# A RWKV attention and MLP kernel on one core: a new issue order, and DMA turns of rows and keys for the last eight tiles

## The chip, the cores and the metric

The kernel runs on one core of a Trainium2 chip. A core has five engines that run side by side, each working through its own queue of instructions in order: TensorE (PE, matrix products, with the loading of its weights shown apart as PEld), VectorE (DVE), ScalarE (ACT), GpSimd (POOL) and SyncE (SP, which here only issues DMAs). Data moves between the device's memory and the on-chip memory by 16 DMA engines. Engines wait for each other through semaphores. The metric is the device time of one execution in microseconds (us); the kernel before took 156.52 us, the median of 3 runs (156.29 to 156.55).

## The reference

Inputs are r, k, v of shape (4, 8, 768, 48), that is batch, heads, time and head width, per-head vectors w and u, a norm weight g and two matrices of an MLP (384×1536 and 1536×384), all in 32 bits.

```python
for t in range(S):
    cur = np.einsum('bhd,bhe->bhde', u[None] * kt, vt)
    y[:, :, t] = np.einsum('bhd,bhde->bhe', rt, state + cur)
    state = w[None, :, :, None] * state + np.einsum('bhd,bhe->bhde', kt, vt)
...
mu, var = mean and variance of x over its 384 columns
xn = (x - mu) / np.sqrt(var + 1e-06) * g_ln
out = x + np.maximum(xn @ w_ch1, 0.0) @ w_ch2
```

Here x is y with the eight heads side by side: 4 × 768 rows of 384.

## The kernel before

**Tiles.** The 768 steps of a sequence are cut into six chunks of 128; with four sequences there are 24 tiles of 128 rows, numbered 0 to 23, each with 384 columns (8 heads of 48). Within a chunk the recurrence is written as a masked product, and a state of 48×48 per head is carried from chunk to chunk.

**Steps.** The kernel is written as small functions, one for each step of the work, and a list, `PLAN`, that calls them. An entry `SK,5,g` calls the function SK for tile 5 on GpSimd; `v` is VectorE, `s` ScalarE, and `-` stands where the engine is fixed. The order of the list is the order in which each engine gets its instructions; between engines only the semaphores count. Nothing else decides the order. For one tile the steps are:

- LK, LR, LV: SP loads keys, rows r and values (192 KB each).
- SK, SR: keys and rows are scaled by powers of w (`Fk`, `Fr`) into `sck` and `scr`, in 16 bits. CV: the values in 16 bits.
- TR: TensorE turns `scr` and `sck` (128×128 transposes, four each) into the bank `tr`; TC (or TCr and TCk for the halves) copies the result to `trs`. For tiles in `K_BY_DMA` TR turns only the rows, TCr copies them, and TKD lets a DMA turn the keys straight into `trs`, issued by SP.
- Q: product of turned rows and keys. AT: TensorE forms the 128×128 products of keys and rows for each head. AM masks them into `A` (AMa and AMb do a half each).
- S: TensorE forms the coefficients of u and, but for the last chunk of a sequence, the increment of the state; for the tiles in `ZPE` it also adds the state before through the identity. CC copies the coefficients, ZU and ZD make the next state `Z`. VB: coefficients times values, on GpSimd.
- Y: TensorE forms the output of the attention from `A`, the values and the state. X adds `Vb`: this is x.
- ST, AG: mean and variance. XN: mean minus x, in 16 bits, `xn`. RS: the inverse root of the variance, used at the end (the sign and g go into the first matrix).
- LT: TensorE turns `xn` (three 128×128 transposes) into the bank `tr`, and XT copies it to `xT`. LTD, which the plan of before does not call, lets a DMA turn `xn` straight into `xT`, issued by SP.
- UP, RL, DN: the MLP. `GROUPS` puts tiles into groups of one or two. UP,16g+m computes four (two, in a group of two) blocks of 128 hidden units of group g for all rows of the group, into one of two banks `hp`; RL takes the positive part into `hT`. DN,4i+d adds the d-th third of the hidden units to the output of tile i; there are three of them a tile. OT multiplies by RS and adds x, STO stores.

**Start.** MW, MP and MI set up constants, WF and ROWSI load w and u (ROWSI by four small DMAs on ScalarE's queue, into `u_p` and `w_p`), LN, WBM, FK and FR make the powers of w, LW1 and SW load and scale the thirds of the first matrix (`w_f`, `w_sb`), IW2 loads those of the second with a cast, on GpSimd's queue. WU and DU are dummy products on TensorE, as many as the number says.

**Buffers.** `SLOTS` says how many buffers each tile has: 10 for each of the three inputs, 3 for `sck`, `scr`, `trs` and `xn`, 4 for `xT` and `hT`. A step that writes into a buffer waits until its last reader is done.

Lines that the prediction names: L203 (products by a vector or tile: SK, SR, Q, ZD), L261 (dummies), L338 (TR), L357 (AT), L367 (AM), L458 and L460 (XN), L477 (TKD), L482 (LT), L497 (UP), L513 and L515 (RL on ScalarE and on VectorE), L525 (DN), L535 (OT), L542 (STO). L198 and L200 are copies on ScalarE and on the other two engines.

Of the kernel before, what the change touches and what calls it, by code (L numbers as in the profile page):

```python
# [10 lines left out]
ACT = mybir.ActivationFunctionType  # L11
ENG = mybir.EngineType

GROUPS = [1, 1, 1, 1, 1, 1, 1, 1, 2, 2, 2, 2, 2, 2, 1, 1, 1, 1]
ZPE = [1, 2, 3]
K_BY_DMA = [18, 19, 20, 21, 22, 23]
SLOTS = {'kf': 10, 'rf': 10, 'vf': 10, 'sck': 3, 'scr': 3, 'vv': 4, 'trs': 3, 'q': 2, 'A': 2, 'cc': 4, 'Z': 3, 'ZS': 2, 'Vb': 3, 'x': 13, 'xn': 3, 'xT': 4, 'hT': 4, 'ot': 3}
PLAN = """
MW,0,v WF,0,- TL,0,s MI,0,g MP,0,v WU,13,- MM,0,g LN,0,s LK,0,- ROWSI,0,s WBM,0,- LV,1,-
LR,0,- FK,0,s CV,1,v FR,0,s SK,0,v LK,1,- SR,0,g LR,1,- SK,1,v DU,18,- TR,0,- UW,0,g  # L20
WL,0,s LK,2,- SR,1,g TCk,0,s LR,2,- TCr,0,s SK,2,g Q,0,v DU,22,- TR,1,- LV,0,- AT,0,-
TCk,1,s SR,2,v LG,0,- LW1,2,- TCr,1,s AMa,0,v CV,0,g UGC,0,s AMb,0,v DU,13,- TR,2,- S,0,-
Q,1,v TC,2,s Y,0,- AT,1,- CC,0,v ZU,0,v LV,2,- AMa,1,v VB,0,g DU,3,- S,1,- SW,7,s
AMb,1,v LW1,1,- SW,8,s IW2,0,g X,0,v SW,6,s DU,13,- AT,2,- Q,2,v Y,1,- CV,2,g ST,0,v
AG,0,v LW1,0,- CC,1,s XN,0,s RS,0,g ZU,1,v SW,5,s SW,3,v DU,16,- LT,0,- VB,1,g XT,0,v
SW,4,s DU,6,- UP,2,- X,1,v S,2,- RL,2,s SW,2,g ST,1,v UP,1,- SW,0,s SW,1,v IW2,2,g
AG,1,v AM,2,v UP,0,- XN,1,s IW2,1,g LK,3,- LT,1,- RL,1,s CC,2,v XT,1,v LR,3,- DU,1,-
Y,2,- RL,0,s VB,2,g ZU,2,v UP,18,- SK,3,v LV,3,- DN,0,- SR,3,v RL,18,s UP,17,- X,2,v
TR,3,- CV,3,g ST,2,v RL,17,s UP,16,- RS,1,g TC,3,v AG,2,v RL,16,s Q,3,v AT,3,- XN,2,v
RS,2,g AM,3,v S,3,- LT,2,- DN,1,- XT,2,s CC,3,s UP,33,- ZU,3,v LK,4,- DN,2,- LV,6,-  # L30
VB,3,g UP,32,- OT,0,v Y,3,- SK,4,v LR,4,- DN,4,- RL,32,v RL,33,s DN,5,- CV,6,s LR,5,-
X,3,v SR,4,v DN,6,- LV,4,- ST,3,v TR,4,- SR,5,g UP,34,- OT,1,v LV,5,- TC,4,s AG,3,v
DN,8,- CV,4,v XN,3,g LK,5,- Q,4,v AT,4,- RL,34,s DN,9,- RS,3,g AM,4,v LK,7,- LT,3,-
S,4,- XT,3,s DN,10,- LK,6,- SK,5,v CC,4,s VB,4,g UP,48,- OT,2,v LR,10,- TR,5,- SK,7,v
UP,49,- SK,6,g ZU,4,v RL,48,s LR,6,- TC,5,v Y,4,- CV,5,s DN,12,- RL,49,v LR,12,- ZD,4,g
AT,5,- X,4,v DN,13,- AM,5,v LR,7,- SR,6,g UP,50,- LV,7,- ST,4,v TR,6,- RL,50,s Q,5,v
SR,7,g Y,5,- AG,4,v STO,1,- TC,6,v S,5,- XN,4,s DN,14,- STO,0,- CC,5,v CV,7,s Q,6,v
VB,5,g LT,4,- LV,11,- AT,6,- XT,4,v S,6,- OT,3,v UP,64,- LV,9,- X,5,v CC,6,s UP,66,-
RS,4,g ST,5,v RL,64,s LR,8,- TR,7,- AM,6,v RL,66,s UP,65,- SR,10,g CV,9,s LK,11,- DN,16,-
AG,5,v RL,65,s TC,7,v RS,5,g Y,6,- LR,9,- XN,5,s DN,17,- ZU,6,v VB,6,g Q,7,v LT,5,-  # L40
LK,8,- DN,18,- XT,5,s AT,7,- X,6,v LK,10,- UP,80,- ST,6,v S,7,- SR,8,v RL,80,s LR,14,-
UP,82,- SK,8,g AM,7,v UP,81,- RL,82,s LK,9,- TR,8,- CC,7,s AG,6,v OT,4,v RL,81,s RS,6,g
Y,7,- LK,14,- TC,8,v XN,6,s DN,20,- VB,7,g CV,11,s ZU,7,v LV,8,- LT,6,- DN,21,- Q,8,v
SR,9,g X,7,v XT,6,s AT,8,- LK,15,- SK,9,v DN,22,- CV,8,s UP,96,- ZD,7,g LV,13,- ST,7,v
AM,8,v TR,9,- RL,96,s SK,10,g STO,2,- S,8,- UP,97,- LR,11,- CC,8,s TC,9,v SR,12,g Y,8,-
OT,5,v RL,97,s TR,10,- STO,4,- Q,9,v AT,9,- VB,8,g LK,12,- TC,10,s AG,7,v UP,98,- ZU,8,v
AM,9,v ZD,8,g S,9,- LV,12,- XN,7,s DN,24,- CC,9,s LT,7,- Q,10,v SK,11,g LR,16,- DN,25,-
ZU,9,v RL,98,s X,8,v AT,10,- XT,7,s LV,15,- DN,26,- ZD,9,g ST,8,v UP,114,- AM,10,v LV,10,-
VB,9,g Y,9,- RL,114,s UP,113,- STO,3,- SR,11,g AG,8,v X,9,v XN,8,s LK,13,- UP,112,- CV,10,s
ST,9,v RS,7,g TR,11,- OT,6,v RL,112,s LR,17,- S,10,- AG,9,v TC,11,v RL,113,s SR,14,g Y,10,-  # L50
DN,28,- CC,10,s LR,15,- SK,13,v CV,12,s XN,9,s VB,10,g LT,8,- AT,11,- ZU,10,v LK,17,- DN,29,-
XT,8,s Q,11,v SK,12,g LT,9,- X,10,v DN,30,- LV,16,- XT,9,s AM,11,v S,11,- UP,130,- RS,8,g
LR,13,- UP,129,- CC,11,v OT,7,v RL,130,s ZD,10,g LK,21,- TR,12,- ST,10,v RL,129,s UP,132,- CV,13,v
VB,11,g TC,12,s SR,15,v LK,19,- UP,131,- RL,132,s Y,11,- STO,6,- SR,13,v AT,12,- RL,131,s LK,16,-
Q,12,v UP,128,- AG,10,v X,11,v XN,10,g S,12,- STO,5,- RL,128,s TR,13,- ST,11,v LK,22,- UP,133,-
CV,15,v SR,16,v SK,15,g DN,32,- TC,13,v RL,133,s LR,22,- DN,33,- AG,11,v AM,12,v XN,11,s Q,13,g
LR,21,- LT,10,- CC,12,s DN,34,- XT,10,s ZU,12,v Y,12,- LV,21,- SK,14,g LT,11,- OT,8,v AT,13,-
S,13,- XT,11,v DN,36,- LR,19,- VB,12,g AM,13,v TR,14,- CV,16,g LR,20,- UP,144,- CC,13,v X,12,v
TC,14,s RS,9,g DN,37,- ZU,13,v LV,14,- RL,144,s ST,12,v ZD,13,g UP,145,- STO,7,- UP,148,- RL,145,s
VB,13,g LV,20,- Q,14,v AT,14,- RL,148,s Y,13,- LK,18,- SK,16,v TR,15,- AG,12,v DN,38,- CV,14,v  # L60
TC,15,v LV,22,- UP,149,- OT,9,v XN,12,s TR,16,- LV,23,- Q,15,v RL,149,s DN,40,- X,13,v SR,19,g
LV,17,- ST,13,v UP,147,- TC,16,s AM,14,v UP,146,- LV,19,- RL,147,s LT,12,- CV,17,g S,14,- AG,13,v
RL,146,s XT,12,v AT,15,- LR,18,- CC,14,v Y,14,- XN,13,s SK,17,v DN,41,- ZU,14,v LR,23,- Q,16,v
LT,13,- DN,42,- VB,14,g AM,15,v XT,13,s LK,20,- S,15,- ZD,14,g UP,163,- OT,10,v STO,8,- UP,162,-
RL,163,s X,14,v SR,18,g DN,44,- SK,18,v SR,17,g UP,160,- ST,14,v STO,9,- AT,16,- RL,162,s CC,15,v
AG,14,v Y,15,- LK,23,- AM,16,v RL,160,s RS,10,g TR,17,- CV,19,s UP,164,- VB,15,g LV,18,- TC,17,v
UP,165,- RL,164,s SR,20,g ZU,15,v DN,45,- Q,17,v XN,14,s STO,10,- ZD,15,g TR,18,- S,16,- X,15,v
TCr,18,s DN,46,- ST,15,v UP,161,- AG,15,v OT,11,v Y,16,- RL,161,s SR,21,v XN,15,g AT,17,- TKD,18,-
CV,20,s LT,14,- CC,16,v DN,48,- XT,14,v RL,165,s VB,16,g LT,15,- DN,49,- XT,15,v Q,18,v RS,11,g
UP,180,- X,16,v STO,11,- ZU,16,v DN,50,- SK,19,g ST,16,v S,17,- TR,19,- OT,12,v UP,176,- RL,180,s  # L70
ZD,16,g AG,16,v CC,17,s DN,52,- AM,17,v VB,17,g UP,178,- RL,176,s TKD,19,- SK,20,g DN,53,- XN,16,v
RL,178,s Y,17,- STO,12,- CV,18,g UP,177,- TCr,19,s AT,18,- CV,21,s Q,19,g TR,20,- RL,177,s X,17,v
UP,181,- AM,18,v DN,54,- RL,181,s SR,22,g UP,179,- OT,13,v TKD,20,- SR,23,g AT,19,- ST,17,v RL,179,s
S,18,- DN,56,- TCr,20,v AG,17,v LT,16,- XN,17,s RS,12,g Y,18,- DN,57,- XT,16,v CC,18,s CV,22,s
ZU,18,v LT,17,- VB,18,g DN,58,- XT,17,v AM,19,v UP,197,- STO,13,- Q,20,g TR,21,- UP,192,- X,18,v
OT,14,v S,19,- AT,20,- RL,197,s SK,22,v DN,60,- TCr,21,s UP,195,- ST,18,v CC,19,s ZU,19,v DN,61,-
VB,19,g STO,14,- AM,20,v Y,19,- RL,195,s ZD,19,g S,20,- DN,62,- X,19,v RL,192,s TR,22,- CV,23,s
Y,20,- OT,15,v SK,21,g UP,194,- ST,19,v CC,20,s UP,193,- TCr,22,v RL,194,s TKD,22,- AG,19,v TR,23,-
VB,20,g RL,193,s UP,196,- AG,18,v XN,18,s TCr,23,v DN,64,- TKD,21,- XN,19,g X,20,v RL,196,s LT,18,-
DN,65,- RS,13,g XT,18,v STO,15,- AT,21,- SK,23,g ZU,20,v LT,19,- DN,66,- XT,19,v AM,21,v ZD,20,g  # L80
UP,212,- UP,209,- RL,212,s Q,21,g OT,16,v Y,21,- UP,208,- RL,209,s AT,22,- S,21,- Q,22,g AM,22,v
DN,68,- CC,21,s UP,213,- VB,21,g ZU,21,v RL,208,s DN,69,- ST,20,v RL,213,s STO,16,- ZD,21,g UP,211,-
# [500 lines left out]
```

## Time and profile before

| | |
|---|---|
| time, median of 3 runs | 156.52 us (156.29 to 156.55) |
| the profiled execution | 156.55 us, span 154.4 us |
| UP (L497) | 648 matmuls, 57.2 us busy |
| DN (L525) | 288 matmuls, 57.1 us busy |
| RL on ScalarE (L513) | 68, 40.0 us busy |
| AM (L367) | 26, 29.1 us busy |
| VB on GpSimd (L420) | 24, 21.6 us busy |
| TR, rows (L338) | 96 transposes, 9.7 us busy |
| moved by DMA | 23.51 MB, 152 GB/s |

The span runs from the first to the last instruction. Busy time counts an engine's instructions; those of TensorE overlap one another, so their sum is longer than the time in which they follow each other. In the slices of the profile each digit stands for a fortieth of the span, 3.86 us, and gives its busy share in tenths. A row of the timeline has start, duration, engine, line, operation, the tiles written and read, the count, and in brackets the idle time before it and what ended that. A row for a line or a tile gives the shortest, the median and the longest duration in ns.

### The profile page before, as it was taken

What the parts mean: (1) busy time and instruction counts of PE and PEld (TensorE: products, weight loads), DVE (VectorE), ACT (ScalarE), POOL (GpSimd) and SP (SyncE); (2) the same over time, 40 slices, a digit from 0 to 9 for tenths busy, and PEclk for the clock granted to TensorE, in tenths of its full rate; (3) what the DMA queues carried; (4) which work ended last, traced back from release to release, by engine and by line L of the source; (5) the groups of instructions that cost most, each with busy time, mean ns of one, the idle gap of its engine ahead of it and who ended that gap; (6) DMA issues with size and microseconds to landing.
All of it is one profiled execution on the core that took longest, in us unless ns stands there. A gap on an engine that the chain in (4) does not pass through costs nothing.

```text
span 154.4 us, 4697 instructions
## 1 busy us (share of the span) xinstructions
PE 146.4 (95%) x1926; PEld 118.6 (77%) x1926; DVE 119.4 (77%) x242; ACT 76.2 (49%) x149; POOL 95.7 (62%) x135
## 2 busy tenths in 40 slices
PE   7689999999899999999999999999999999999990
PEld 4488788868677887979688878877778778878770
DVE  2256989789998999999999999797797769734211
ACT  4526884434155747657535746356455244143330
POOL 3182665356749499995693698798766968333200
PEclk9999999999999999999999999999999999999998
DMA  4999999999999999989899897132153051102111
GB/s 82 192 182 354 349 200 206 210 177 212 226 200 188 199 255 179 257 170 232 170 243 208 176 261 107 51 89 34 51 87 87 0 89 51 51 20 82 56 56 51
DMA packets 84487, 23.51 MB, mean 152 GB/s; under 512 B 79857, under 2 KB 82930, under 8 KB 84466
## 3 DMA queue, kind: packets, MB, share of 16 engines
q1 hardware_dynamic: 83202, 22.03, 64.5%
q0 software_dynamic: 432, 1.18, 4.2%
q8 instruction: 15, 0.25, 0.7%
q10 hardware_dynamic: 832, 0.00, 0.3%
q14 instruction: 6, 0.05, 0.1%
HBM read 18.88 MB, written 4.72 MB: 153 GB/s over the span
## 4 chain that ended last, share of the span: by engine, by line
PE 73%; DVE 16%; DMA 3%; ACT 2%; issue 2%; SPq 1%; POOL 1%; POOLq 0%; DVEq 0%; ACTq 0%
PE o L525 27%; PE hp L497 26%; PE tr L338 5%; PE at L357 4%; DVE A L367 4%; DMA rf<-in_r_dram 3%; PE tr L482 3%; DVE scr L203 2%; PE y L438 2%; PE s L401 2%; PE y L430 2%; PE o L261 2%; DVE x L445 2%; PE s L388 1%; DVE stats L448 1%
## 5 line engine op out<-in xcount | busy, mean ns | idle before, releaser
L513 ACT ACTIVATE hT<-hp 128x512 bf16<-128x512 f32 x68 | 40.0, 597 | 49.5 <-PE hp L497 48.9
L497 PE MATMUL hp<-xT,w_sb 128*128 128x128 bf16 (+1 forms) x648 | 57.2, 237 | 0.3 <-ACT w_sb L306 0.2
L525 PE MATMUL o<-w_sb,hT 128*128 128x384 bf16 x288 | 57.1, 326 | 0.2 <-DVE hT L515 0.2
L497 PEld LDWEIGHTS <-w_sb 128*128 128x128 bf16 x648 | 49.4, 113 | 4.4 <-ACT w_sb L306 0.4
L525 PEld LDWEIGHTS <-hT 128*128 128x128 bf16 x288 | 25.3, 98 | 11.6 <-DVE hT L515 0.4
L367 DVE TENSOR_TENSOR A<-at,mask 128x1024 bf16<-128x1024 f32 (+1 forms) x26 | 29.1, 1127 | 3.3 <-PE at L357 3.3
L420 POOL TENSOR_TENSOR Vb<-vf,cc 128x384 f32<-128x384 f32 x24 | 21.6, 898 | 12.6 <-ACT cc L198 6.7
L203 POOL TENSOR_TENSOR scr<-rf,Fr 128x384 bf16<-128x384 f32 x16 | 16.2, 1019 | 11.7 <-DMA rf<-in_r_dram 8.2
L535 DVE SCALAR_TENSOR_TENSOR ot<-o,rs,x 128x384 f32<-128x384 f32 x24 | 14.7, 611 | 10.3 <-PE o L525 10.2
L445 DVE TENSOR_TENSOR x<-y,Vb 128x384 f32<-128x384 f32 x24 | 13.1, 547 | 4.2 <-POOL Vb L420 3.1
L203 POOL TENSOR_TENSOR Z<-ZS,WLZ 128x384 bf16<-128x384 f32 x13 | 13.6, 1048 | 2.5 <-DVE ZS L414 2.3
L198 ACT COPY trs<-tr 128x512 bf16<-128x512 bf16 (+1 forms) x13 | 10.0, 782 | 10.5 <-PE tr L338 10.5
L448 DVE BATCH_NORM_STATS2 stats<-x 128x6 f32<-128x384 f32 x24 | 13.3, 554 | 0.4
L203 POOL TENSOR_TENSOR sck<-kf,Fk 128x384 bf16<-128x384 f32 x12 | 12.6, 1046 | 0.3 <-PE s L401 0.3
L469 POOL TENSOR_TENSOR rs<-rs,expo 128x1 f32<-128x1 f32 (+1 forms) x18 | 10.9, 603 | 1.5
L338 PE MATMUL tr<-ident,scr 128*128 128x128 bf16 x96 | 9.7, 227 | 1.9 <-POOL scr L203 1.9
L261 PE MATMUL o<-warm 128*128 128x128 bf16 x105 | 10.3, 269 | 1.0 <-DVE warm L226 1.0
L203 DVE TENSOR_TENSOR sck<-kf,Fk 128x384 bf16<-128x384 f32 x12 | 9.6, 799 | 1.4 <-DMA kf<-in_k_dram 1.4
L203 DVE TENSOR_TENSOR q<-trs 128x512 bf16<-128x512 bf16 x18 | 8.8, 489 | 2.4 <-ACT trs L198 2.4
L261 PEld LDWEIGHTS <-warm 128*128 128x128 bf16 x105 | 8.7, 124 | 2.4 <-issue 1.3
L458 ACT ACTIVATE xn<-x,mv 128x384 bf16<-128x384 f32 x15 | 9.2, 613 | 2.5 <-DVE mv L452 2.5
L357 PE MATMUL at<-trs 48*128 48x128 bf16 x192 | 9.8, 222 | 0.4 <-DVE trs L200 0.3
(66 smaller groups left out, 180.2 us busy)
## 6 DMA issues: line engine op xcount, KB each, us to landing
kf<-in_k_dram SPq DMA_DIRECT2D x24, 192.0 KB, 3.9
vf<-in_v_dram SPq DMA_DIRECT2D x24, 192.0 KB, 4.1
rf<-in_r_dram SPq DMA_DIRECT2D x24, 192.0 KB, 3.9
out_dram<-ot SPq DMA_DIRECT2D x24, 192.0 KB, 2.5
w_f<-in_moe_w_ch_dram SPq DMA_DIRECT2D x3, 768.0 KB, 7.3
w_sb<-in_moe_w_ch_dram POOLq DMA_DIRECT2D x3, 384.0 KB, 6.5
trs<-sck SPq DMA_TRANSPOSE x6, 3.6
u_p<-in_u_dram ACTq DMA_DIRECT2D x2, 0.8 KB, 3.1
```

Of the source, the lines that this page charges most:

```text
L203: engines[e].tensor_tensor(out=out, in0=in0, in1=in1, op=ALU.mult)
L261: nc.tensor.matmul(out=warm_ps[0][:, :P], lhsT=warm[:], rhs=warm[:], start=True, stop=True)
L338: nc.tensor.transpose(out=t[:, a * HP + q, :], in_=flat[:, q, :], identity=ident[:])
L357: nc.tensor.matmul(out=t[:, par, q, :], lhsT=trs(i)[p0 : p0 + D, 1, q, :], rhs=trs(i)[p0 : p0 + D, 0, q, :], start=True, stop=True,)
L367: nc.vector.tensor_tensor(out=AA(i)[:, a:b].rearrange("p e q t -> p (e q) t"), in0=psum["at", i][:, a:b].rearrange("p e q t -> p (e q) t") ...
L420: nc.gpsimd.tensor_tensor(out=Vb(i)[:].rearrange("p (h d) -> p h d", h=H), in0=vf(i)[:], in1=cc(i)[:].unsqueeze(2).to_broadcast([P, H, D]) ...
L445: nc.vector.tensor_tensor(out=xx(i)[:], in0=psum["y", i][:, :C], in1=Vb(i)[:], op=ALU.add)
L448: nc.vector.bn_stats(out=stats[i % 4][:], in_=xx(i)[:])
L497: nc.tensor.matmul(out=t[:, a * gw : (a + 1) * gw], lhsT=w1_sb[n][kc][:, fb::FB], rhs=xT(g)[:, kc, :gw], start=(kc == 0), stop=(kc == CK - 1),
L513: nc.scalar.activation(out=o, in_=s, func=ACT.Relu)
L525: nc.tensor.matmul(out=psum["o", i][:, :C], lhsT=hT(g)[:, fk, j * P : (j + 1) * P], rhs=w2_sb[d][:, a, :], start=(fk == 0), stop=(fk == FK ...
L535: nc.vector.scalar_tensor_tensor(out=ot(i)[:], in0=psum["o", i][:, :C], scalar=rs[g][:, j : j + 1], in1=xx(i)[:], op0=ALU.mult, op1=ALU.add,)
```

## The change

Only the three constants at the head of the file change: `GROUPS`, `K_BY_DMA` and `PLAN`. All functions stay as they are, and so does ROWSI, the small loads of w and u on ScalarE's queue. The text that comes with the change says that the order was searched with a lock between VectorE and GpSimd.

- `GROUPS`: tiles 0 to 5 alone, 6 to 21 in eight groups of two, 22 and 23 alone (before: 0 to 7 alone, 8 to 19 in six groups of two, 20 to 23 alone).
- `K_BY_DMA`: tiles 16 to 23 (before 18 to 23), so two more TKD.
- `PLAN`: for tiles 16 to 23 LTD stands in place of LT and XT. The whole order is another, the engines of many steps change, and the dummies are 111 in ten entries and WU, where they were 105.

Steps by engine, before and after, where the count differs:

| step | before | after |
|---|---|---|
| XT | 14 VectorE, 10 ScalarE | 1 VectorE, 15 ScalarE |
| TC | 10 VectorE, 6 ScalarE | 1 VectorE, 14 ScalarE |
| RL | 68 ScalarE, 4 VectorE | 60 ScalarE, 12 VectorE |
| XN | 15 ScalarE, 6 GpSimd, 3 VectorE | 18 ScalarE, 3 GpSimd, 3 VectorE |
| SR | 16 GpSimd, 8 VectorE | 14 GpSimd, 10 VectorE |
| Q | 18 VectorE, 6 GpSimd | 19 VectorE, 5 GpSimd |
| CC | 16 ScalarE, 8 VectorE | 20 ScalarE, 4 VectorE |
| CV | 13 ScalarE, 6 GpSimd, 5 VectorE | 11 ScalarE, 8 GpSimd, 5 VectorE |
| SW | 6 ScalarE, 2 VectorE, 1 GpSimd | 5 ScalarE, 3 VectorE, 1 GpSimd |

```diff
-GROUPS = [1, 1, 1, 1, 1, 1, 1, 1, 2, 2, 2, 2, 2, 2, 1, 1, 1, 1]
+GROUPS = [1, 1, 1, 1, 1, 1, 2, 2, 2, 2, 2, 2, 2, 2, 1, 1]
-K_BY_DMA = [18, 19, 20, 21, 22, 23]
+K_BY_DMA = [16, 17, 18, 19, 20, 21, 22, 23]
 PLAN = """
-MW,0,v WF,0,- TL,0,s MI,0,g MP,0,v WU,13,- MM,0,g LN,0,s LK,0,- ROWSI,0,s WBM,0,- LV,1,-
-LR,0,- FK,0,s CV,1,v FR,0,s SK,0,v LK,1,- SR,0,g LR,1,- SK,1,v DU,18,- TR,0,- UW,0,g
...
+MW,0,v WF,0,- TL,0,s MI,0,g WU,13,- MM,0,g LN,0,s MP,0,v LR,1,- ROWSI,0,s WBM,0,- LR,0,-
+LK,0,- FK,0,s FR,0,s LK,1,- SK,0,v SR,0,v LK,2,- SK,1,v DU,18,- TR,0,- UW,0,g WL,0,s
+LV,0,- SR,1,g TCk,0,v TCr,0,v LR,2,- SK,2,g DU,13,- TR,1,- Q,0,v CV,0,s AT,0,- TC,1,s
...
+RS,0,g DU,10,- AT,2,- ZU,1,v LR,3,- SW,3,s LT,0,- AM,2,v S,2,- VB,1,g SW,0,s LW1,2,-
+SW,1,g SW,2,s X,1,v XT,0,s ST,1,v DU,14,- Y,2,- SR,3,g CC,2,s UP,1,- AG,1,v XN,1,s
+LK,3,- ZU,2,v UP,0,- IW2,1,g RL,1,s SW,8,v IW2,0,g LT,1,- LK,4,- SW,6,v IW2,2,g SK,3,v
...
+RL,161,s UP,162,- X,18,v Q,19,g TCr,20,s OT,13,v UP,165,- STO,12,- RL,162,s AG,17,v ZU,18,v TKD,21,-
+DN,56,- Q,20,g XN,17,s ST,18,v AT,20,- RL,165,s TR,21,- AG,18,v Y,19,- SR,23,g TCr,21,s DN,57,-
+AM,20,v LTD,17,- RS,11,g TR,22,- S,19,- XN,18,s DN,58,- TCr,22,v CV,23,g CC,19,s SK,22,v AT,21,-
+VB,19,g UP,176,- ZU,19,v UP,178,- OT,14,v RL,176,s LTD,18,- ZD,19,g X,19,v S,20,- DN,60,- CC,20,s
...
+UP,195,- LTD,20,- ST,21,v DN,70,- AG,21,v STO,16,- UP,196,- RS,13,g XN,21,s OT,17,v S,22,- DN,72,-
+RL,196,v RL,195,s Y,22,- CC,22,s ZU,22,v DN,73,- VB,22,g LTD,21,- S,23,- DN,74,- X,22,v ZD,22,g
```

The two functions that turn by DMA, unchanged:

```python
def LTD(i, e):
    g, j, _ = group_of[i]
    nc.sync.dma_start_transpose(out=xT(g)[:, :, j * P : (j + 1) * P], in_=xn(i)[:])

def TKD(i, e):
    flat = sck(i)[:].rearrange("p h d -> p (h d)")
    nc.sync.dma_start_transpose(out=trs(i)[:, 1], in_=flat)
```

## The prediction

> **What bounds the kernel now.** I read the busy table and the slices first, then the timeline of TensorE, then the chain of waits, and last the rows of single lines and tiles.
>
> ```profile
> span 154.4 us, 4697 instructions
> ...
> PE 146.4 (95%) x1926; PEld 118.6 (77%) x1926; DVE 119.4 (77%) x242; ACT 76.2 (49%) x149; POOL 95.7 (62%) x135
> ...
> DVE  2256989789998999999999999797797769734211
> ...
> DMA  4999999999999999989899897132153051102111
> ```
>
> TensorE is busy nearly throughout; VectorE is full from slice 9 to 24, and the DMA engines are full until slice 24 (about 95 us) and nearly empty after it. A busy TensorE may still be losing time, so I went to its timeline:
>
> ```profile
> 8.13 0.61 PE L338 MATMUL tr<-ident,scr 128*128 128x128 bf16 x4 [1.85 <-POOL scr L203]
> ...
> 8.96 2.55 PE L261 MATMUL o<-warm 128*128 128x128 bf16 x22
> ...
> 19.43 0.83 PE L497 MATMUL hp<-xT,w_sb 128*128 128x128 bf16 x12
> ...
> 121.79 1.47 PE L497 MATMUL hp<-xT,w_sb 128*128 128x256 bf16 x12
> 123.10 0.33 PE L430 MATMUL y<-Z,trs 128*128 128x96 bf16 x4
> ...
> 143.31 0.33 PE L482 MATMUL tr<-ident,xn 128*128 128x128 bf16 x3
> 143.48 0.81 PE L525 MATMUL o<-w_sb,hT 128*128 128x384 bf16 x4
> 144.13 1.50 PE L497 MATMUL hp<-xT,w_sb 128*128 128x128 bf16 x24
> 145.47 2.11 PE L525 MATMUL o<-w_sb,hT 128*128 128x384 bf16 x12
> 147.42 1.50 PE L497 MATMUL hp<-xT,w_sb 128*128 128x128 bf16 x24
> 148.76 2.11 PE L525 MATMUL o<-w_sb,hT 128*128 128x384 bf16 x12
> ```
>
> The price of a step is read from one start to the next: LT 0.17, DN 0.65, UP 0.667 in a group of one (1.34 for two) and 0.655 in a group of two (1.31 for two). In the same way TR is 0.45 (0.225 without the key), AT 0.33, S 0.10 plus 0.165 for the state and 0.16 for the identity, Y 0.205 plus 0.17, a dummy 0.056. The whole program is then TR 18×0.45 + 6×0.225 = 9.45, AT 7.9, S 6.2, Y 8.3, LT 24×0.17 = 4.1, UP 36×0.667 + 36×0.655 = 47.6, DN 72×0.65 = 46.8, dummies 105×0.056 = 5.9: 136.2 us. The last DN starts at 150.06, and 135.6 of the sum lies ahead of it, so 14.5 us are lost. Laid along the timeline, 9.8 are lost by 19.43, 10.9 by 31, 12.0 by 43, 13.3 by 77, 14.5 at the end. Some 1.7 of these are AT's own (24 times about 0.07 ahead of its first matmul), and would stay. So the time is set by TensorE's sum, the first 20 us, and about 3 us of waits in between. Where those come from, the chain shows:
>
> ```profile
> 36.71 0.62 DVE ot L535
> 37.33 1.30 DVE sck L203
> 38.63 0.26 DVE ZS L414
> ...
> 39.02 0.67 DVE trs L200
> 39.70 0.60 DVE hT L515
> ```
>
> VectorE is late, and with an operation that took 1.30 where it can take 0.55:
>
> ```profile
> L203 DVE TENSOR_TENSOR q<-trs x18: 402/418/976, 10.3 to 99.5; 128x512 bf16<-128x512 bf16 x18
> ...
> L203 DVE TENSOR_TENSOR sck<-kf,Fk x12: 549/669/1385, 5.6 to 112.8; 128x384 bf16<-128x384 f32 x12
> ```
>
> **The change, part by part.** Four terms.
>
> *TensorE's sum.* The keys of tiles 16 and 17 leave TR (−2×0.225 = −0.45), LT goes for eight tiles (−8×0.17 = −1.36), four more tiles are in groups of two (−12×0.012 = −0.14), and six dummies are added (+0.34). Sum −1.6: 134.6 us of work. TensorE has no slack to hide this in after 43 us, so it counts in full, unless a new wait takes it back.
>
> *The start.* The loads now come r1, r0, k0, k1. The third load of before was there at 7.0 (POOL begins at 7.09), so SK,0 and then SR,0 on VectorE (0.55 each, more beside POOL) put TR,0 at about 8.3 instead of 8.13. Only 13 dummies at 0.107 (the slow rate of the 22 in the timeline) stand ahead of TR,1, which gives AT,0 at 11.5 instead of 12.30. The lead shrinks: AT,1 14.0, S,1 15.6, AG,0 17.25, XN,0 17.9, LT,0 18.0 (18.64 before). Then XT,0 stands on ScalarE behind three scalings of weights (0.7 each) and ends at 20.3, where VectorE had it done by 19.4. The first UP starts at 20.35 with 9.9 of the sum done: 10.45 lost against 9.8. It goes on with UP,18 at 26.4 (10.9 lost); the loads of w2 follow SR,3 on POOL, so issue at 21 to 22.5 and, with 6.5 to land, arrive near DN,0 at 27 to 28; DN,2 at 31.3 has lost 11.2, against 10.9. I take +0.4. Bounds: −0.6 if the lead at AT,0 is kept, +1.8 if the last third of w1 and w2 are another 1.4 late.
>
> *Waits in the middle.* VectorE gives up thirteen XT (0.36 each) and nine TC (0.68), and takes eight RL (0.66), two SR, a Q and a scaling: its busy sum falls by about 3.5. Counted in pieces of 8 us of TensorE's sum, the old order gives VectorE 9.1, 8.6 and 8.7 us in the three pieces from 40 to 64; the new one 8.2, 7.9 and 7.4. Its worst pieces are 8.9 (72 to 80) and 8.5 (88 to 96). The excess over the shortest forms (12×0.25 for sck, 8×0.22 for scr, 18×0.09 for q) is 6.4 us of VectorE, and it falls where POOL runs beside it; an order that knows of it could halve it. Of the 3.6 us lost after 31, 1.5 are AT's; I take 1.2 of the other 2.1. Bounds: all 2.1 gained, or 0.5 lost, since ScalarE gets six more us of work and its RL now queue behind copies.
>
> *The turns by DMA.* An LT ran behind XN at once; a turned row needs SP to issue it and the DMA to land, and UP waits for it. The nearest row is the key's:
>
> ```profile
> L477 SPq DMA_TRANSPOSE trs<-sck x6: 1190/1212/1947, 92.3 to 123.8; - x6
> ...
> DMA to landing us min/median/max: 2.4/3.6/4.3
> ```
>
> Sixteen of these at 1.2 hold SP for 19 us out of some 60, with stores between them; the DMA engines are nearly empty there, so throughput is no issue, lateness is. I followed each chain in TensorE's bare sum. UP,176 (tiles 16, 17) is due at 98.0; VectorE, with 23.3 us of work in the 22.3 before it, ends AG,17 at 95.4, XN,17 on ScalarE takes 0.61, LTD,17 is issued at 96.1: 1.9 of slack. UP,193 (18, 19): LTD,19 at 103.0 for 106.0, slack 3.0. UP,208 (20, 21): AG,21 waits behind RL,194 and ST,21, LTD,21 at 113.15 for 116.55, slack 3.4. Groups 22 and 23 have 4 and more. With landing L the stalls are L−1.9, L−3.0 and L−3.4 where positive: 0.5 at 2.4, 2.5 at 3.6, 4.6 at 4.3. A row tile is three quarters of a key tile (128×384 against 128×512); scaled so, 3.6 becomes 2.7, a stall of 0.8. Between 0.8 and 2.5 I take 1.7, as nothing shows which part of the landing is size. The keys' own turns stall less: AT,16 and AT,20 come out even to 1 us late, and what they lose, the rows behind them gain as slack. Bounds 0 and 4.6.
>
> The page DMA: Bandwidth & Descriptors of the Trainium skill (section Latency and other measured facts) gives a DMA transpose 261 GB/s; by that a quarter of 131 kB is an estimated 0.13 us, so nearly all of the 3.6 would be fixed. By the page the stalls would be 2.2 instead of 1.7 and the total 156.3. No run here shows a row's turn yet.
>
> Sum, against the profiled execution's 156.55 (span 154.4 and 2.15 around it; it stands at the top of the three runs, median 156.52): 156.55 − 1.6 + 0.4 − 1.2 + 1.7 = 155.85.
>
> **The rivals.** *The turns are hidden* (155.85 − 1.7 = 154.1): for it, the six turns of before made nobody wait, and SP ran far ahead of its place in the list; against it, those chains started at a load, these start at the end of VectorE's. *The turned rows become the bound* (slower): at UP,176, UP,193 and UP,208 TensorE, in order, waits with all its DN behind. At 4.3 that is 4.6, total 158.8; break-even with the other terms (−2.4) is a landing of 3.6, the median of before. For it: LTD stands behind stores and keys on one queue. Against: most weight of the landing may be size. *The start or VectorE's relief fails*: with a start of +1.8, 157.2; with no relief in the middle, 157.05. For it: ScalarE has 8.3 us of work in the 8 in which the first UP comes. *The new order changes nothing that counts*: the work saved comes back as waits, 156.5.
>
> **How the numbers follow.** A measurement of this kernel tells about 0.2%, 0.3 us, from no change. Forecast (154.9 to 156.2) 0.33; turns hidden, below that, 0.17; nothing that counts (156.2 to 156.8) 0.11; rows as the bound 0.24; start or relief failing 0.15. Faster 0.5, same 0.11, slower 0.39. The likeliest case alone reaches from 154.9 to 156.2; with the others the range is 153.5 (all bounds good but the start) to 158.9 (the slower rival).
>
> **What would show it.** Right: no LT and no key turn on TensorE after tile 15; the first UP near 20.3; VectorE's sck and scr nearer their 0.55; short gaps of TensorE, 0.5 to 2 each, ahead of UP,176, UP,193 and UP,208 released by a DMA; the last DN ending 0.7 us earlier. Wrong: landings of rows above 4 us; a gap of over 1 us ahead of DN,0; waits of AT for keys; or VectorE ending AG,17 early, so that the rows land ahead of their UP.

## The result and the profile after

The new order is slower: 163.86 us (median of 4 runs, 163.32 to 164.80) against 156.54 us of the kernel before on the same chip, a ratio of 1.048 (95% interval 1.0414 to 1.0545). Its profiled execution took 163.56 us. On other chips the kernel before took 157.8 to 158.3 us, so the experiments are given as ratios to the kernel before on the same chip; executions more than 1.5% above the fastest of their kernel are left out of the ratios, which are therefore not always quotients of medians.

The page of after, with the busy table, the slices and the shares of the chain of waits:

```profile
span 161.8 us, 4521 instructions
...
PE 146.3 (90%) x1828; PEld 118.3 (73%) x1828; DVE 116.9 (72%) x228; ACT 81.2 (50%) x157; POOL 90.4 (56%) x127
...
DVE  2359859008589999899998899899878687743341
...
PEclk9999999659999999999999999999999999999999
...
DMA  4996999995659989899998989530824302312211
...
PE 66%; DMA 14%; SPq 9%; POOL 4%; DVE 3%; issue 1%; ACT 0%; DVEq 0%; POOLq 0%
```

TensorE is as busy as before over a span that is 7.4 us longer. Slices 7 and 8 (28 to 36 us) are the odd ones: VectorE has two slices of nothing, and TensorE's granted clock falls to 0.6 and 0.5. The DMA engines now have holes in slice 3 and in slices 9 to 11, where before they were full. TensorE's timeline, read as in the prediction:

```profile
20.90 1.50 PE L496 MATMUL hp<-xT,w_sb 128*128 128x128 bf16 x24 [1.35 <-ACT xT L197]
...
24.27 0.86 PE L496 MATMUL hp<-xT,w_sb 128*128 128x128 bf16 x12 [0.81 <-DVE w_sb L307]
...
26.85 0.40 PE L356 MATMUL at<-trs 48*128 48x128 bf16 x8
32.37 0.61 PE L337 MATMUL tr<-ident,scr 128*128 128x128 bf16 x4 [5.12 <-POOL scr L202]
...
117.17 0.40 PE L356 MATMUL at<-trs 48*128 48x128 bf16 x8 [0.29 <-DMA trs<-sck]
...
139.82 0.85 PE L496 MATMUL hp<-xT,w_sb 128*128 128x256 bf16 x6 [0.25 <-DMA xT<-xn]
```

(Line numbers of after are one lower than before; those of the experiments are 18 or 19 lower, since their plan is written in fewer lines.) The row at 32.37 is TR,4. It waited 5.12 us for the scaled rows, and behind it, in TensorE's order, stood UP,18 and the first DN. GpSimd's and SP's timelines say why the rows were late:

```profile
20.94 1.87 POOL L312 DMA_DIRECT2D w_sb<-in_moe_w_ch_dram  x3
...
31.32 0.99 POOL L202 TENSOR_TENSOR scr<-rf,Fr 128x384 bf16<-128x384 f32 x1 [6.21 <-DMA rf<-in_r_dram]
```

```profile
9.29 3.80 SPq L220 DMA_DIRECT2D g_p<-in_moe_g_ln_dram  x1
13.14 1.67 SPq L298 DMA_DIRECT2D w_f<-in_moe_w_ch_dram  x1
...
16.00 3.06 SPq L315 DMA_DIRECT2D kf<-in_k_dram  x2
19.11 3.25 SPq L318 DMA_DIRECT2D rf<-in_r_dram  x1
```

SP was held 3.80 us by the small load of g (0.91 before), then 3.06 over two loads of keys, and 3.25 by the rows of tile 4 themselves, which it put in between 19.11 and 22.36. GpSimd had put in the three thirds of w2 from 20.94. Between 24 and 26 us the DMA engines served these:

```profile
q0 software_dynamic: 145, 0.40, 105.1%
q1 hardware_dynamic: 5, 0.00, 0.4%
```

The columns are packets, MB and the share of the 16 engines; q0 is GpSimd's queue, q1 that of SP. The thirds landed at 26.1, 28.1 and 30.5, the rows of tile 4 at 31.2: 12.1 us after their issue, where the median is 3.7.

Lost time is again the real start of a step minus TensorE's bare sum ahead of it:

| up to | before | after |
|---|---|---|
| UP,1 and UP,2, the first blocks of the MLP | 9.8 (at 19.43) | 11.0 (at 20.90), 12.0 (at 24.27) |
| TR,4 | 11.0 (at 32.56) | 17.3 (at 32.37) |
| S,3 | 10.9 (at 26.92) | 19.1 (at 36.08) |
| last DN | 14.5 (at 150.06) | 23.3 (at 157.28) |

TR,4 starts at nearly the same time in both, but in before more work stands ahead of it, 21.6 us of the sum against 15.1, and nothing waits for it:

```profile
32.56 0.39 PE L338 MATMUL tr<-ident,scr 128*128 128x128 bf16 x4
```

The sum itself fell from 136.2 to 134.6, so 23.3 − 14.5 − 1.6 gives the 7.2 us by which the last DN starts later.

### The profile page after: what moved, and what is told of

Read it like the earlier page. It is cut to its first block, busy times and chain, and to the rows that moved or that the text cites. A ratio compares the mean times of both kernels' runs of the same rounds, so it can differ in the third digit from the quotient of the medians.

```text
span 161.8 us, 4521 instructions
## 1 busy us (share of the span) xinstructions
PE 146.3 (90%) x1828; PEld 118.3 (73%) x1828; DVE 116.9 (72%) x228; ACT 81.2 (50%) x157; POOL 90.4 (56%) x127
## 3 DMA queue, kind: packets, MB, share of 16 engines
q0 software_dynamic: 432, 1.18, 4.1%
## 4 chain that ended last, share of the span: by engine, by line
PE 66%; DMA 14%; SPq 9%; POOL 4%; DVE 3%; issue 1%; ACT 0%; DVEq 0%; POOLq 0%
PE o L524 25%; PE hp L496 25%; DMA rf<-in_r_dram 10%; PE tr L337 4%; PE at L356 3%; DMA trs<-sck 2%; SPq L220 2%; DMA xT<-xn 2%; PE y L437 2%; SPq L298 2%; PE y L429 2%; SPq L315 2%; DVE q L202 2%; PE s L400 2%; PE tr L481 2%; POOL scr L202 1%
## 5 line engine op out<-in xcount | busy, mean ns | idle before, releaser
L496 PE MATMUL hp<-xT,w_sb 128*128 128x128 bf16 (+1 forms) x576 | 56.5, 248 | 2.4 <-ACT xT L197 1.3
L496 PEld LDWEIGHTS <-w_sb 128*128 128x128 bf16 x576 | 48.3, 115 | 5.5 <-issue 1.4
L512 ACT ACTIVATE hT<-hp 128x512 bf16<-128x512 f32 x60 | 35.5, 599 | 32.3 <-PE hp L496 31.8
L197 ACT COPY trs<-tr 128x1024 bf16<-128x1024 bf16 (+1 forms) x20 | 17.6, 882 | 14.1 <-PE tr L337 14.0
L202 POOL TENSOR_TENSOR scr<-rf,Fr 128x384 bf16<-128x384 f32 x14 | 14.5, 1033 | 6.6 <-DMA rf<-in_r_dram 6.2
L465 POOL TENSOR_SCALAR rs<-mv 128x1 f32<-128x1 f32 (+1 forms) x16 | 4.1, 257 | 22.3 <-DVE mv L451 21.7
L457 ACT ACTIVATE xn<-x,mv 128x384 bf16<-128x384 f32 x18 | 11.1, 617 | 6.2 <-issue 5.2
L337 PEld LDWEIGHTS <-scr 128*128 128x128 bf16 x96 | 7.0, 102 | 7.4 <-POOL scr L202 5.3
L202 DVE TENSOR_TENSOR q<-trs 128x512 bf16<-128x512 bf16 x19 | 11.1, 589 | 0.5 <-ACT trs L197 0.4
L202 DVE TENSOR_TENSOR sck<-kf,Fk 128x384 bf16<-128x384 f32 x12 | 7.8, 660 | 4.5 <-DMA kf<-in_k_dram 4.4
```

Of the source, the lines that this page charges most:

```text
L197: nc.scalar.copy(out=out, in_=in_)
L202: engines[e].tensor_tensor(out=out, in0=in0, in1=in1, op=ALU.mult)
L337: nc.tensor.transpose(out=t[:, a * HP + q, :], in_=flat[:, q, :], identity=ident[:])
L457: nc.scalar.activation(out=xn(i)[:], in_=xx(i)[:], func=ACT.Identity, bias=mean, scale=-1.0)
L496: nc.tensor.matmul(out=t[:, a * gw : (a + 1) * gw], lhsT=w1_sb[n][kc][:, fb::FB], rhs=xT(g)[:, kc, :gw], start=(kc == 0), stop=(kc == CK - 1),
L512: nc.scalar.activation(out=o, in_=s, func=ACT.Relu)
```

## The experiments

Each is the changed kernel with an edited order, unless it says otherwise. A "lost" time is that of its profiled execution.

| run | ratio to before (95%) | lost at the last DN |
|---|---|---|
| the change | 1.048 (1.0414 to 1.0545) | 23.3 |
| e1_g_early | none formed | 19.5 |
| e2_r4_early | 1.0243 (1.0187 to 1.0299) | 22.8 |
| e3_g_and_r4_early | 1.0258 (1.0200 to 1.0317) | 22.0 |
| e4_dummies_in_gap | 1.0249 (1.0178 to 1.0320) | 16.1 |
| e10_w2_behind_r4 | one run, 165.45 us | 25.2 |
| e13_w2_behind_r4_dummies | one run, 164.06 us | 17.4 |
| e8_tile4_later | 1.0050 (1.0017 to 1.0084) | 18.4 |
| e11_tile4_later_no_row_turns | 1.0185 (1.0094 to 1.0276) | 18.1 |
| e5_before_with_dma_turns | 1.0310 (1.0242 to 1.0379) | 23.0 |
| h1_old_start_new_rest | 1.0116 (1.0033 to 1.0199) | |
| h1_no_row_turns | 1.0281 (1.0218 to 1.0344) | |
| h2_old_start_longer | 0.9952 (0.9910 to 0.9994) | 18.25 |

### Is it the one late load? e1, e2, e3

The load of g is moved ahead of the first issued third of w1 (e1), the rows of tile 4 ahead of its last third (e2), or both (e3):

```diff
 e1
-LW1,1,- AMb,0,v
+LG,0,- LW1,1,- AMb,0,v
...
 e2
-SW,0,s LW1,2,- SW,1,g
+SW,0,s LR,4,- LW1,2,- SW,1,g
```

> The changed kernel with one load moved: the load of g (three numbers of 4 bytes for each of 128 partitions), which held SP for 3.80 us from 9.29 while the DMA engines ran dry at 13 to 16 us, goes ahead of the first third of w1, as in the order before. Theory A (the loss is made by late loads at the start, one cause being this hold of SP): the second and third thirds of w1 land about 3 us earlier, the waits of UP,1 (1.5) and UP,2 (1.0) go, row tile 4 lands up to 3 us earlier, so 163.6 falls by 2.5 to 5.5, to about 160. Theory B (the DMA engines are full until 95 us, so a load moved only shifts the wait to the next one; the loss is the new order's as a whole): 163 to 164.

> The changed kernel with one load moved: row tile 4 goes ahead of the last third of w1 instead of behind it and two key tiles. In the changed kernel it is issued at 19.1 to 22.4, lands at 31.2, after the three loads of w2 that GpSimd issues at 20.9 to 22.8, and TR,4 waits 5.1 us for it. Theory A: the row tile lands near 20, the wait of 5.1 and the half rate of TensorE behind it (about 1.7) go, UP,2 is up to 1 us later: 163.6 - 6.8 + 1 = about 157.5. Theory B: the wait goes to another tile of the same stage, 162 or more.

> Both moves of the two kernels beside it. Theory A: with both causes gone the start is as long as in the order before or shorter, about 155 to 156.5, so at or below the kernel before (156.5). Theory B: above 161.

In e1 SP was held all the same: the load now in that place, a third of w1, took 3.72 us from 9.76. So the hold is not g's own; the hole of the DMA engines in slice 3, though, is gone with the move (the digit is 9, in after 6). The rows of tile 4 landed at 26.9 and TR,4 waited 2.2. The four runs lie apart (159.72, and 162.30 to 163.66), and its 19.5 lost are those of the shortest. In e2 the rows landed at 20.6 and TR,4 did not wait, but the next loads stood behind w2 in their place: the values of tile 3 landed at 32.1. TensorE in e2:

```profile
24.43 0.86 PE L478 MATMUL hp<-xT,w_sb 128*128 128x128 bf16 x12 [1.12 <-DVE w_sb L289]
...
29.42 0.81 PE L506 MATMUL o<-w_sb,hT 128*128 128x384 bf16 x4 [0.79 <-DMA w_sb<-in_moe_w_ch_dram]
...
32.73 0.33 PE L382 MATMUL s<-vv,sck 128*128 128x96 bf16 x4 [2.06 <-POOL vv L181]
```

Three shorter waits came in place of one long one, and e3 lost 22.0 (its wait for the values of tile 3 was 2.0). About half of the loss stayed, so moving one load ahead is not the remedy.

### What does the idle gap itself cost? e4, e10, e13

e4 puts 88 dummies ahead of TR,4. e10 issues w2 only behind the scaling of tile 4's rows; e13 is e10 with 115 dummies ahead of DN,0.

```diff
 e4
-RS,2,g TR,4,-
+RS,2,g DU,88,- TR,4,-
...
 e10
-UP,0,- IW2,1,g RL,1,s SW,8,v IW2,0,g LT,1,- LK,4,- SW,6,v IW2,2,g SK,3,v
+UP,0,- RL,1,s SW,8,v LT,1,- LK,4,- SW,6,v SK,3,v
...
-SR,4,g UP,16,-
+SR,4,g IW2,1,g IW2,0,g IW2,2,g UP,16,-
...
 e13, against e10
-AM,3,v DN,0,-
+AM,3,v DU,115,- DN,0,-
```

> The changed kernel with 88 more dummy products ahead of TR,4, which fill the 5.1 us in which TensorE waits for row tile 4 (88 times 0.056 is 4.9). Theory A with the clock (the idle gap brings TensorE to half rate until about 36 us, 1.7 us lost): the wait stays, the half rate goes, 163.6 falls to about 161.9. If the slow products behind the gap have another cause: 163.6 or, where the dummies outlast the wait, a little more.

> The changed kernel with the three loads of w2 issued behind SR,4 on GpSimd, so that they can not run ahead of row tile 4. If the DMA engines' throughput bounds the start, the wait only moves: TR,4 waits under 2 us, DN,0 then waits 3 to 5 us for w2, and the time is within 2 us of the changed kernel's. If the place of the one load was all: the 5.1 us and the half rate go, about 157 on the chip of the first runs.

> The kernel with w2 behind SR,4, in which TensorE waited 6.8 us ahead of DN,0 and then ran at half rate until about 41 us, with 115 more dummies ahead of DN,0 to fill that wait. If the idle gap brings the half rate: the granted clock stays at 1.00 and the 2.8 us lost between DN,0 and UP,32 fall below 0.8, so about 2 us less than that kernel. If the half rate comes from something else, it stays.

e4 showed something else than it was made for. In its profiled execution SP was 1.2 us ahead and had put in all of tile 4's rows by 20.38, just as GpSimd began with w2 at 20.16; they landed at 23.75 and nobody waited. Three profiles of the same loads, in order:

| | rows of tile 4 put in | w2 from | its thirds land | the rows land |
|---|---|---|---|---|
| e4 | 17.88 to 20.38 | 20.16 | 25.6, 28.4, 30.4 | 23.75 |
| e1 | 18.74 to 21.34 | 20.61 | 26.1, 28.8, 30.7 | 26.9 |
| after | 19.11 to 22.36 | 20.94 | 26.1, 28.1, 30.5 | 31.2 |

In these three profiles about a microsecond of SP's lead goes with over 7 us of landing: the rows come in ahead of the first third of w2, just behind it, or behind all three. e4 without its 4.9 us of dummies would not simply be that much shorter: the values of tile 3 landed only at 30.2, S,3 behind them started at 31.8, and without the dummies TensorE would, as far as this trace tells, have waited there instead. Its other runs took 162.77 to 164.11 us and have no trace.

e10 also shows what delays the rows. With w2 held back they landed at 25.07, 6.2 us after their issue (in e13 6.3), and not 12.1. TR,4 waited 0.4, but DN,0 waited 6.6 for w2: the wait only moves. DN,0 in e10, then in e13:

```profile
34.18 1.44 PE L506 MATMUL o<-w_sb,hT 128*128 128x384 bf16 x4 [6.63 <-DMA w_sb<-in_moe_w_ch_dram]
```

```profile
35.51 0.82 PE L506 MATMUL o<-w_sb,hT 128*128 128x384 bf16 x4 [1.08 <-DMA w_sb<-in_moe_w_ch_dram]
```

The windows of e10, then of e13 (columns: from and to, length, busy time and count of PE, PEld, DVE, ACT and POOL, the granted clock, the DMA share, GB/s):

```profile
32.00:34.00 2.00, 0.00 (x0) 0.00 (x0) 0.00 (x0) 0.00 (x0) 0.00 (x0) 0.50 1.09 206
34.00:36.00 2.00, 1.82 (x12) 1.13 (x12) 0.00 (x0) 0.03 (x1) 0.00 (x0) 0.50 1.12 218
36.00:38.00 2.00, 2.00 (x27) 1.50 (x25) 0.72 (x3) 0.45 (x1) 0.83 (x1) 0.50 0.87 177
38.00:40.00 2.00, 2.00 (x13) 1.40 (x12) 1.97 (x3) 0.00 (x0) 0.00 (x0) 0.50 0.66 124
40.00:42.00 2.00, 2.00 (x31) 1.76 (x29) 0.72 (x3) 1.19 (x2) 0.00 (x0) 0.99 0.00 0
```

```profile
32.00:34.00 2.00, 2.00 (x40) 2.00 (x38) 0.00 (x0) 0.00 (x0) 0.00 (x0) 1.00 1.10 209
34.00:36.00 2.00, 0.92 (x11) 0.56 (x9) 0.00 (x0) 0.00 (x0) 0.00 (x0) 1.00 1.07 204
36.00:38.00 2.00, 2.00 (x38) 1.59 (x36) 0.96 (x3) 0.48 (x1) 0.78 (x1) 1.00 1.18 238
38.00:40.00 2.00, 2.00 (x30) 1.75 (x28) 1.97 (x4) 0.83 (x2) 0.04 (x1) 1.00 0.54 109
```

Both wait for the same third of w2. Left idle, TensorE comes back at a granted clock of 0.50 and keeps it until 40 us; with dummies the clock stays at 1.00. From the start of DN,0 to that of the last DN e10 takes 124.98 us and e13 122.23: the gap's aftermath costs 2.75 us beside the gap, 2.65 of it by DN,2. Each is a single run. In total e13 gained less, because its third of w2 landed 1.3 us later (35.46 against 34.14) and DN,0 still waited 1.08 behind the dummies.

### Is it that tile 4 is asked for too early? e8

The steps of tile 4 go later: SK and SR behind DN,1, TR, TC, Q, AT and AM behind DN,2, S behind DN,4 and Y behind DN,5. The values of tile 3 go ahead of the keys and rows of tile 4, and g as in e1. The diff shows TensorE's order that results.

```diff
-TR,3,- UP,17,- UP,16,- AT,3,- TR,4,- UP,18,- DN,0,- LT,2,- S,3,- Y,3,- AT,4,- DN,1,- UP,34,- UP,32,- DN,2,-
+TR,3,- UP,17,- UP,16,- AT,3,- UP,18,- DN,0,- LT,2,- S,3,- Y,3,- DN,1,- UP,34,- UP,32,- DN,2,- TR,4,- UP,33,- AT,4,-
```

> The changed kernel, with the work on tile 4 asked for later: SR,4, TR,4, TC,4, Q,4, AT,4, AM,4, S,4 and Y,4 stand behind DN,2 instead of ahead of UP,18 and DN,0; the values of tile 3 are loaded ahead of keys and rows of tile 4, and g ahead of the first third of w1. Nothing else differs. Theory A (the loss is that the new order asks for tile 4 at a time when the DMA engines, full since 2 us, are still bringing w2): no wait over 1 us and no half rate before 40 us, 5.5 to 7.5 us less than the changed kernel, a ratio to before of 0.99 to 1.005. Theory B (the rest of the new order is slower too): still 1.02 or more.

The ratio falls from 1.048 to 1.005, some 6.7 us of 156.5, with the turns, the groups and the rest of the order as they were. The rows of tile 4 still came nearly as late, at 30.75 (31.2 in after), but nobody waits for them, since TR,4 now has 20.0 us of the sum ahead of it. The values of tile 3 landed at 22.6 (32.1 in after). The first DN and TR,4 of e8:

```profile
28.02 0.81 PE L506 MATMUL o<-w_sb,hT 128*128 128x384 bf16 x4 [1.90 <-DMA w_sb<-in_moe_w_ch_dram]
...
32.28 0.39 PE L319 MATMUL tr<-ident,scr 128*128 128x128 bf16 x4
```

What is left of the waits of TensorE:

```profile
PE o L506 <- DMA w_sb<-in_moe_w_ch_dram: 1.9, 1, 1.9
PE tr L319 <- DVE scr L184: 1.3, 1, 1.3
...
PE hp L478 <- DMA xT<-xn: 0.5, 1, 0.5
```

The columns are the total in us, the number of times, and the longest. No gap is over 2 us, the granted clock is 1.00 throughout, and 10.1 are lost at UP,1. The wait for w2 is more than the 1 us that theory A allowed. e8 moves three things at once, and what each is worth was not separated. Its ratio rests on six of twelve executions; by the median of all twelve it is 1.1% above before.

### What do the turns by DMA cost? e5, e11, h1

e5 is the kernel before, order and groups unchanged, with two more keys and the eight rows turned by DMA. e11 is e8, and h1_no_row_turns is h1_old_start_new_rest, with LT and XT in place of LTD. In e11 LT,19 and XT,19 come behind UP,193, so that the MLP of tiles 18 and 19 reads tile 19's rows before they are written. In h1_no_row_turns TCr,23 stands right behind TR,23.

```diff
 e5, against before
-K_BY_DMA = [18, 19, 20, 21, 22, 23]
+K_BY_DMA = [16, 17, 18, 19, 20, 21, 22, 23]
...
-RL,196,s LT,18,- DN,65,-
+RL,196,s LTD,18,- DN,65,-
...
 e11, against e8
-VB,18,g DN,54,- LTD,16,- ST,17,v
+VB,18,g DN,54,- LT,16,- XT,16,s ST,17,v
```

> The kernel before in its own order and groups, with the DMA part of the change alone: keys of tiles 16 and 17 and rows of tiles 16 to 23 turned by DMA, the XT of these tiles left out. If the turns are hidden: 1.8 us less work on TensorE, ratio 0.988 to 0.992. If their waits take back about half: 0.993 to 0.998. If the turns are what made the changed kernel slow: 1.01 or more.

> The kernel beside it (tile 4 later), with the turned rows of tiles 16 to 23 made by TensorE again: LT and XT on ScalarE at the places of LTD. It prices the row turns alone. If they are hidden, TensorE has 1.36 us more to do and the time rises by 0.9 to 1.4. If waits for their landing (0.3 to 0.4 us each ahead of UP,176 and UP,208 in the changed kernel's trace) take it back, it rises by 0.3 to 0.8. If the prediction's slower rival holds, it falls by 1 or more.

> The kernel beside it (old start, new rest) with the rows of tiles 16 to 23 turned by TensorE again (LT at the places of LTD, XT on ScalarE, TCr,23 right behind TR,23). It prices the row turns where the order gives them lead. In the changed kernel's trace TensorE waits 0.3 us in all for turned rows, so with 1.36 us of LT back on TensorE the time should rise by 0.8 to 1.4 (ratio 0.005 to 0.009 higher). If the row turns cost what the prediction took (1.7): it stays the same or falls.

In the old order the turns cost 3.1%. TensorE's timeline of e5:

```profile
113.91 0.82 PE L478 MATMUL hp<-xT,w_sb 128*128 128x256 bf16 x6 [1.18 <-DMA xT<-xn]
...
127.00 1.47 PE L478 MATMUL hp<-xT,w_sb 128*128 128x256 bf16 x12 [2.26 <-DMA xT<-xn]
...
136.33 0.86 PE L478 MATMUL hp<-xT,w_sb 128*128 128x128 bf16 x12 [0.47 <-DMA xT<-xn]
...
150.82 1.53 PE L478 MATMUL hp<-xT,w_sb 128*128 128x128 bf16 x24 [1.12 <-DMA xT<-xn]
```

These four waits are 5.0 of the 8.5 us that it lost more than before; the rest are shorter ones (1.0 for w2, 0.7 and 0.5 ahead of TR,17 and TR,4). The old order has LT just ahead of its UP and gives a DMA little lead. In the new order they are a gain: taking the row turns out costs 1.35% (1.0185 against 1.0050) in one pair and 1.65% (1.0281 against 1.0116) in the other, 2.1 to 2.6 us by the medians of before, though the intervals allow 0.1 to 2.6% in the first pair and 0.2 to 3.1% in the second. The profiled executions of the first pair lie only 1.0 us apart (159.73 and 158.71), so the gain of the row turns is about 1 to 2 us, near the 1.36 us of eight LT. The copies XT come back on ScalarE, and in e11 TR,22 waits 0.57 for one of them.

### Is the rest of the new order better? h1, h2

Both take the order of before up to a point and the steps that remain in the order of after: h1 up to DN,6 (about 33 us), h2 up to DN,14 (about 44 us).

```diff
 the seam of h2
 STO,1,- TC,6,v S,5,- XN,4,s DN,14,-
-STO,0,- CC,5,v CV,7,s Q,6,v VB,5,g
+LK,8,- STO,0,- RS,4,g LR,9,- CC,5,s VB,5,g CV,7,s STO,2,- Q,6,v
```

> The order before up to and with DN,6 (about the first 31 us: tiles 0 to 4 begun, w1 and w2 loaded), and then all steps not yet done in the changed kernel's order, with its groups and its DMA turns. Theory A (the changed kernel loses at the start alone): the start loses 10.9 us as before, the rest 4.3 as in the changed kernel, with 134.3 of work on TensorE in place of 136.2: 1 to 1.5 us under the kernel before, ratio 0.990 to 0.995. Theory B (the rest of the new order is slower too): 1.01 or more.

> As the first, with the order before up to and with DN,14 (about 47 us), so that the loads, too, come in the old order until then. Theory A: within 0.5 us of the first. If the stage from 31 to 47 us is where the new order relieves VectorE (the prediction's term of 1.2): 0.5 to 1.2 us slower than the first.

h2 is faster than both kernels, barely: 0.9952 (0.9910 to 0.9994), by seven of its twelve executions. The span of its profiled execution, the clock and the DMA engines in its slices:

```profile
span 156.4 us, 4512 instructions
...
PEclk9999999999999999999999999999999999999999
DMA  4999999999999698999979969316542312213111
```

It has no hole in the DMA engines' slices before the seam, no fall of the clock, and 12.35 lost at 43 us (12.0 before). From there it loses 5.9 to the end, where before, profiled on another chip, lost 2.5, in waits of 0.2 to 0.8: LT,5 0.80, AT,20 0.62, UP,208 0.50, LT,12 0.48, S,17 0.46, S,13 0.39, Y,20 0.36. In this execution these short waits give back what the smaller sum saves, and more; how h2 still comes out ahead by 0.5% is not seen in it (158.16 us, the longest of those in the ratio). h1, with the seam inside the loaded start, came out at 1.0116, where theory B had put it, but from two of six executions; its runs scatter widely (159.4 to 175.1 us), and its profile is not used. h2, 1.6% under h1, fits neither theory.

## Why the prediction was wrong

The forecast was 155.85 with 153.5 to 158.9 around it (by its own terms the lower end comes to 153.25). By its four terms, against the profiled execution:

**TensorE's sum, −1.6: right.** The instructions are those counted, and their prices hold where the clock is 1.00.

**The start, +0.4 with a bound of +1.8: the step that failed.** It is +8.2 (19.1 lost against 10.9). The prediction saw the first UP at 20.35 and the trace has 20.90, with 1.35 of waiting for XT,0's copy, which it named; the last third of w1 added another 1.0 within its own bound of 1.4. The sentence that failed is the next, "It goes on with UP,18 at 26.4". It asked of the loads only when w2 would arrive, and took for granted that the rows of tile 4, whose TR stands ahead of UP,18, would be there: it has no time for their landing. They landed at 31.2, and TR,4 waited 5.12. The prediction counted neither the three thirds of w2 that GpSimd puts into the same 16 engines nor SP being held (3.80 by g, 3.06 over two loads of keys, 3.25 by the rows themselves). That it is this, and not the turns, e8 and e10 show together: with w2 held back the rows land after 6.2 us and not 12.1, and with tile 4 asked for later its rows come nearly as late, 6.7 us are gone, and the turns are still there. Why SP is held was not found.

The second part of the +8.2 was in no term: after 5.1 us without work the granted clock is 0.50 from 29.5 to 36.4 us. By the table this is 1.8 us between TR,4 and S,3 (17.3 to 19.1); e10 and e13 show the same for a gap of 6.6 us, at 2.75. In windows of after:

```profile
28.00:30.00 2.00, 0.00 (x0) 0.00 (x0) 0.52 (x1) 0.00 (x0) 0.00 (x0) 0.88 1.08 208
30.00:32.00 2.00, 0.00 (x0) 0.00 (x0) 0.00 (x0) 0.00 (x0) 0.68 (x1) 0.50 1.19 239
32.00:34.00 2.00, 1.63 (x16) 1.63 (x17) 0.00 (x0) 0.56 (x1) 1.51 (x4) 0.50 1.07 202
34.00:36.00 2.00, 2.00 (x14) 1.33 (x12) 0.00 (x0) 1.05 (x2) 1.15 (x1) 0.50 1.10 216
36.00:38.00 2.00, 2.00 (x36) 1.57 (x35) 1.12 (x3) 0.48 (x1) 0.83 (x1) 0.91 1.14 225
```

**Waits in the middle, −1.2: not there.** After 36 us 4.3 are lost. About 1.4 are AT's own and 0.7 the turns'; the remaining 2.2 are what before lost there, 2.1. VectorE's busy sum fell by 2.5 (119.4 to 116.9), short of the 3.5 counted, and its long products only traded: `sck` came down from 799 to 660 ns in the mean, `q` went up from 489 to 589; the cause was not tested. And new short waits, for ScalarE's copies, for GpSimd's `Z` and for `ZS`, took the place of the old ones. That ScalarE's longer queue causes these was not tested.

**The turns by DMA, +1.7: too high by 1.0, and the slack was right in two places of three.** UP,208 waited 0.3, AT,20 0.3 to 0.45, UP,176 and UP,193 nothing: about 0.7. From the issue of the last LTD to the start of the UP, less any wait, the trace has 3.4 us at UP,193 and 3.4 at UP,208 (3.0 and 3.4 forecast), but 3.5 at UP,176 where 1.9 was forecast: there the rows landed ahead of their UP, which the prediction itself named as a sign of being wrong. The landings:

```profile
L476 SPq DMA_TRANSPOSE trs<-sck x8: 1188/1196/1656, 96.5 to 126.7; - x8
...
DMA to landing us min/median/max: 2.4/2.9/4.0
```

```profile
L472 SPq DMA_TRANSPOSE xT<-xn x8: 1179/1183/1187, 111.7 to 145.8; - x8
...
DMA to landing us min/median/max: 2.3/2.3/3.7
```

A row turn holds SP for 1.18 us, as a key does; its shortest landing is 2.3 against 2.4. So little of it is size, and the prediction's scaling by three quarters was wrong as a reason; the key's own median fell too, from 3.6 to 2.9. The Trainium skill's page DMA: Bandwidth & Descriptors (section Latency and other measured facts) gives a DMA transpose 261 GB/s, by which the quarter in size is an estimated 0.13 us; the trace agrees that it counts for little (2.3 against 2.4). The 3.5 that the prediction built on it, 3.6 less 0.13, is nevertheless 1.2 above the 2.3 measured, farther off than the scaled 2.7.

**The rivals.** "Turned rows become the bound" was the slower side with the largest chance, and it did not happen here, because 3.4 to 3.5 us of slack were there at each of the three places, against a median landing of 2.3. As a mechanism it is real: e5 has it at 5.0 us. "The start or VectorE's relief fails" named both terms that did fail, but priced the start from w1 and w2 alone. The sum of the terms as measured, −1.6 + 8.2 + 0.1 + 0.7, is 7.4, about the 7.2 by which the last DN is later and the 7.4 between the spans.

**What stays open.** Why the rest of the new order loses 5.9 us behind 43 in h2 where before lost 2.5 is told only by the list of its waits. What holds SP for 3 to 4 us around 9.3 to 9.8 us was not tried apart from moving g. And in how many executions of after tile 4's rows lose the race is known only by the times: its four runs are within 1%.

## What to carry to other kernels

While the DMA engines are full, a load's landing is not its place on its own queue: count also the transfers that other queues put in before the issue ends (here the large ones went ahead), and ask of each step in an in-order list whether its load can be there. Work that needs a late load should stand behind work that does not, and if a gap of microseconds can't be avoided, its price is the gap and, where the clock falls, the slower clock after it. A step that is moved onto a DMA is free only where the order gives it the lead that a landing takes, here 2.3 to 3.7 us; the turns of the rows gained 1 to 2 us in one order, and with two more keys they lost 5 in the other.

## What the hardware showed that was not expected

**Large packets against small ones.** By the shares in these windows w2's packets take 210 to 240 ns each, those of a row tile (192 bytes) about 15 where they are alone (30 to 32 us) and 26 beside w2. In 24 to 26 us of after 145 of the first were served and 5 of the second. The Trainium skill's page DMA: Bandwidth & Descriptors (section Queues, rings and completion order) says that an engine takes turns between its queues packet by packet, a packet holding some 9 to 17 descriptors. In the next 2 us the counts are one against one, with no such bundling of the small ones:

```profile
q0 software_dynamic: 140, 0.38, 96.4%
q1 hardware_dynamic: 139, 0.03, 11.5%
```

One for one is no rule either: 22 to 24 us has 44 to 1064, 28 to 30 us 103 to 734. Neither these nor the 145 to 5 follow from the page's rule, and no run here explains them.

**The clock falls after a gap of some 2 us.** The Trainium skill's page TensorE: Matmul & The Clock Gate (Part 1) gives half clock after an idle window of about 3.4 us, counted in windows that run freely. In the windows of after the fall comes about 2.3 us after the last product; a gap of 2.2 us was enough in e1 (0.50 for about 3.4 us, from just after the work had come back), and one of 2.1 in e2 and of 2.0 in e3, with shorter ones ahead of them. One of 1.9 in e8 was not, nor one of 2.26 in e5 (ahead of 127.0). The page's free-running windows may account for e5: counted on from the rise of its clock at 13.33 in steps of 3.415 us (half of the 6.83 from 29.52 to 36.35 in after), a window ends at an estimated 126.0 and cuts that gap into 1.3 and 1.0 us, where the gaps that brought a fall lay for 2.0 us or more within one window. That is inferred, and not the whole rule: in h1_no_row_turns the clock fell at 41.64 with no single gap over 1.1 us ahead of it. How long it stays agrees with the page: about 3.4 us in e1, e2 and e3, twice that in after.
